# Retention and a multiplicative feed-forward layer on one core: where three pairs of weight sums are given out within one block

## The chip, the cores and the metric

The kernel runs on one core of a Trainium2 chip. The metric is the device time of one execution in microseconds (us). An execution agrees with the next within some tenths of a per cent, so differences under about 0.5% need several runs to be seen.

## The reference

All of it is float32. For 8 batches, 8 heads, 576 positions and 64 numbers per head, retention is computed without a softmax, and its output is the input of a feed-forward layer that multiplies two projections.

```python
scores = matmul(q, k.transpose(0, 1, 3, 2)) / sqrt(64)
ret = scores * where(i >= j, gamma[h] ** (i - j), 0)      # gamma = 1 - 2 ** (-5 - h)
x = matmul(ret, v)  ->  (4608 tokens, 512)
out = ((x @ w1) * (x @ w2)) @ w3 @ w_out                   # 512 -> 1024 -> 1024 -> 512
```

## The kernel before

**Attention in chunks.** Batches are taken in four pairs, and each sequence of 576 positions in five chunks (64 and four of 128). A step g is one chunk of one pair. `load` and `load_blocks` bring q, k and v; `front_blocks` turns q and k into qT and kT with VectorE transposes (L190); `score` (L233) multiplies them and VectorE applies the mask to the products (L236, tile pm, four instructions); `state` (L255) keeps the running sum over chunks; `pv_state` (L274) and `pv` (L299) make the output, which ScalarE copies into xT tiles of 384 tokens. The decays are multiplied onto q and v by GpSimd or ScalarE (L181, L202, L204).

**The feed-forward layer.** The two last weights are multiplied once into w3o. A token tile passes four `up` blocks, one for each quarter of the 1024 hidden columns, in which w1 and w2 are handled together, and then `down` blocks with w3o. Both are in a fast form with seven products for a 2 x 2 partition of the matrices instead of eight. Its operands are blocks of the weights (A11, A12, A22, kept in tile wA) and sums of them (S3 also in wA; S1, S2, S4 in wS), and blocks and sums of the tokens (B and T). There is one wA and one wS for each half of the hidden columns; these are the "first half" (wA0, wS0) and the "second half" (wA1, wS1).

**One up block** (`up`, L511 to L568) makes seven products in the order A11 x B11, S2 x T2, S3 x T3, S1 x T1, A22 x -T4, A12 x B21, S4 x B22. Each is eight matmuls (L528). A12 x B21 is added in PSUM onto the first product, and S4 x B22 onto the fourth. ScalarE copies the first product to tile c (L546, and L561 after A12 x B21), VectorE adds the others to c in five additions (`plus`, L533). The third addition reads the bank of S1 x T1; the fifth reads the same bank after S4 x B22. At the end VectorE multiplies the two projections into tile ab (L566).

**The down block** (`down`, L632 to L722, matmuls in L651) makes products 1, 7, 2, 6, 5, 4, 3 in this order. Its token sums S3, S2, S1 (L614, L618, L620) are put ahead of it, and S4 (L699) is made after product 2. VectorE combines the products (L701, L655), and the results are stored from L729. Product 2 is added onto product 1 in PSUM, and product 3 onto product 5, behind VectorE's addition of product 5.

**Work that is given out.** Lists of small jobs are filled ahead of a block, and each addition of a block hands one job from `aside` and one from `spread` to the engines:

```python
        def plus(ps, to, sb):
            nc.vector.tensor_add(c[:, to], ps, c[:, sb])
            convert(conv.pop(0) if isinstance(conv, list) else conv)
            for extra in (aside, spread):
                if extra:
                    extra.pop(0)()
```

The instructions of an engine stand in the order in which this code calls them. `flush` hands out all that is left in `spread`.

**Weight forms.** The first four token tiles use the seven-product form once. The later eight use it twice over (`up2`, matmuls in L1060), with weights that are read from device memory into a ring of slots (tile ra, `next_forms`, L961). `weight_forms(h, second)` makes these weights in place for half h, after the last up block that reads them. The first sums are one job, the second sums three. Each such job is a pair of VectorE instructions (L891), one on wA and one on wS. After the first sums, a job sends the results to the memory tile kept: four DMAs of wA (L901) and one of wS (L904), issued by GpSimd. The second sums change wA and wS again, so they wait until those sends have read them. After them a job sends the rest through SP's queue, eleven DMAs (L901, L904, L907). The first ring slot is laid over wA0, so its load stands behind these sends in SP's queue.

**The list around the change.** The four up blocks of the last tile that uses the one-level form, three down blocks and the jobs between them stand in the list `todo` (L1198 to L1202). `work(n)` runs the next n blocks from it, and after each block all jobs that follow it in the list. Up blocks 0 and 1 of the tile read the first half's weights, blocks 2 and 3 the second half's. The first half's first sums and their sends are given out in block 2, its second sums in block 3, the "last up block". In block 3, `aside` holds the transpose of the next chunk's query, an empty entry, the transpose of its key (L190), and then the down block's L614 and L618; L620 follows after the block.

Of the kernel before, what the change touches and what calls it, by code (L numbers as in the profile page):

```python
# [19 lines left out]
def kernel(  # L20
# [66 lines left out]
    def load(g, names, engine=nc.sync):  # L87
        i, c = divmod(g, NC)
        sz = sizes[c]
        src = {"k": k, "q": q, "v": v}  # L90
        for nm in names:
            t = pools["ld"].tile([P, 2 * H, D], F32, tag="ld_" + nm, name="ld_" + nm)
            engine.dma_start(
                t[:sz], src[nm][2 * i:2 * i + 2, :, starts[c]:starts[c] + sz, :].rearrange("b h p d -> p (b h) d"))
            live[nm, g] = t
# [64 lines left out]
    def load_blocks(g, nm):  # L160

        i, c = divmod(g, NC)
        n = sizes[c] // BL
        t = pools["ld"].tile([P, 2 * NP, P // BL, BL], F32, tag="ld_q", name="bl_" + nm)
        src = {"k": k, "q": q}[nm][2 * i:2 * i + 2].rearrange("b (p a) s d -> a (b p) s d", a=2)
        for a in range(2):
            for f in range(D // BL):
                part = (a * (D // BL) + f) * BL
                for m in range(n):
                    s0 = starts[c] + m * BL  # L170
                    nc.sync.dma_start(t[part:part + BL, :, m, :],
                                      src[a, :, s0:s0 + BL, f * BL:(f + 1) * BL].rearrange("m r x -> r m x"))
        live["bl_" + nm, g] = t

    def scale_blocks(g):
        c = g % NC
        n, n0 = sizes[c] // BL, starts[c] // BL
        t = live["bl_q", g]
        for b in range(2):
            part = t[:, b * NP:(b + 1) * NP, :n, :]  # L180
            nc.gpsimd.tensor_tensor(  # L181
                out=part, in0=part, in1=gqs[:, :, n0:n0 + n].unsqueeze(3).to_broadcast([P, NP, n, BL]),
                op=ALU.mult)

    def front_blocks(g, names="kq"):
        c = g % NC
        n = sizes[c] // BL
        for nm in names:
            dst = pools["fr"].tile([P, 2, NP, P], F32, tag=nm + "T", name=nm + "T", bufs=1 if nm == "k" else 2)
            nc.vector.transpose(  # L190
                dst[:, :, :, :sizes[c]].rearrange("p b m (n x) -> p (b m) n x", x=BL),
                live["bl_" + nm, g][:, :, :n, :])
            live[nm + "T", g] = dst

    def scale(g, nm, scalar=False, engine=nc.gpsimd):
        c = g % NC
        sz = sizes[c]
        t, gam = live[nm, g], {"q": gq, "v": gk}[nm]
        t = t[:sz].rearrange("p (b h) d -> p b h d", b=2)
        if scalar:  # L200
            for h in range(H) if scalar is True else scalar:
                nc.scalar.mul(t[:, :, h, :], t[:, :, h, :], gam[:sz, c, h:h + 1])  # L202
            return
        engine.tensor_tensor(  # L204
            out=t, in0=t, in1=gam[:sz, c].unsqueeze(1).unsqueeze(3).to_broadcast([sz, 2, H, D]), op=ALU.mult)

    def front(g, names="kq"):
        c = g % NC
        sz = sizes[c]
        for nm in names:  # L210
            src = live[nm, g]
            dst = pools["fr"].tile([P, 2, NP, P], F32, tag=nm + "T", name=nm + "T",
                                   bufs=1 if nm == "k" and g >= NC else 2)
            for b in range(2):
                tp = acc.tile([P, NP, P], F32, tag="acc", name="tp")
                for p in range(NP):
                    h = b * H + 2 * p
                    nc.tensor.transpose(tp[:, p, :sz],  # L218
                                        src[:sz, h:h + 2, :].rearrange("p a d -> p (a d)"),
                                        ident[:sz, :sz])  # L220
                nc.scalar.copy(dst[:, b, :, :sz], tp[:, :, :sz])
            live[nm + "T", g] = dst
# [55 lines left out]
    def pv(g):  # L278

        if ("xps", g) not in live:  # L280
            pv_state(g)
        i, c = divmod(g, NC)
        sz = sizes[c]
        live["x", g] = True
        vs, pm, banks = live["v", g], live["pm", g], live["xps", g]

        parts = []
        for n in range(NB):
            lo, hi = max(starts[c], n * TB), min(starts[c] + sz, (n + 1) * TB)
            if lo < hi:  # L290
                m = i * NB + n
                if ("xT", m) not in live:
                    live["xT", m] = xps[m % 4 == 3].tile([P, NP, 2, TB], F32, tag="xT", name="xT")
                parts.append((live["xT", m], lo - n * TB, lo - starts[c], hi - lo))
        for m, (b, n) in enumerate(bank_order):
            for r in range(2):
                for half in range(2):
                    p, j = 2 * r + n, half ^ r
                    nc.tensor.matmul(banks[r][heads[half], b, n, :sz], vs[:sz, b * H + 2 * p + j, :],  # L299
                                     pm[:sz, b, j, p, :sz], start=(c == 0 and m == 0), stop=True,  # L300
                                     skip_group_check=True)

        def evict():
            for x, to, fr, n in parts:
                for r in range(2):
                    nc.scalar.copy(  # L306
                        x[:, 2 * r:2 * r + 2, :, to:to + n].rearrange("p n b s -> p b n s"),
                        banks[r][:, :, :, fr:fr + n])

        return evict  # L310
# [261 lines left out]
    aside, owed, spread, beside, loads = [], [], [], [], []  # L572
# [256 lines left out]
    todo = [(0, 1, 2), (0, 0, 3), (0, 1, 3)] + [(0, 2, fp) for fp in range(NQ - 1)]  # L829
# [38 lines left out]
    todo = [(down, (0, 0), (0, 1)), (down, (0, 2), (1, 2))]  # L868
# [266 lines left out]
    def work(n):  # L1135
        while n > 0 and todo:
            fn, *args = todo.pop(0)

            nxt = next((x for x in todo if x[0] in real), None)
            if nxt and nxt[0] is down:  # L1140
                if fn is down:
                    args.append(nxt[1:])
                else:
                    ahead(*nxt[1:], 1 if fn is up2 else 3)
            if g == G and not todo:
                fn(*args, last=True)
            else:
                fn(*args)
            n -= 1
            while todo and todo[0][0] not in real:  # L1150
                todo.pop(0)[0]()
# [11 lines left out]
    for g in first_pair:  # L1163
        n = (1, 1, 2, 2)[g - NC]
        if not in_blocks[g + 2]:
            load(g + 2, "k")
            load_blocks(g + 2, "q")
        scale(g + 1, "v")
        if not in_blocks[g + 1]:
            front(g + 1, "k")  # L1170
            front_blocks(g + 1, "q")
        half = (n + 1) // 2
        if in_blocks[g + 1]:
            scale_blocks(g + 1)
            work(n - 1)
            aside.extend([lambda: front_blocks(g + 1, "q"), lambda: None, lambda: front_blocks(g + 1, "k")])
            work(1)
            while aside:
                aside.pop(0)()
            half = 0  # L1180
        if in_blocks[g + 2] and g + 2 < 2 * NC:
            load_blocks(g + 2, "q")
            load_blocks(g + 2, "k")
        work(half)
        if g < NC + 2:

            weight_forms(g - NC, False)[2]()
        pv(g)()
        load(g + 2, "v", nc.scalar if in_blocks[g + 2] else nc.sync)
        if in_blocks[g + 2] and (g + 2) % NC != NC - 1:  # L1190
            load(g + 2, "k")
        state(g + 1)
        score(g + 1)
        if not in_blocks[g + 2]:
            scale_blocks(g + 2)
        if g == NC + 1:
            list(strassen_tokens(1, 0))
            forms = [(lambda h=h, second=second: spread.extend(weight_forms(h, second)[:None if second else 2]),)  # L1198
                     for h in halves for second in (False, True)]
            ups = [(up, 1, 0, fp) for fp in range(NQ)]  # L1200
            todo.extend([*ups[:2], forms[0], ups[2], forms[1], ups[3], (flush,), forms[2], (flush,), (down, (1, 0), (1, 1)),
                         (down, (2, 2), (3, 2)), (open_second,), (down, (3, 0), (3, 1))])  # L1202
        if not in_blocks[g + 1]:
            work(n // 2)
# [116 lines left out]
```

## Time and profile before

| | |
|---|---|
| median of the runs shown (834.87, 837.93, 837.85) | 837.85 us |
| the profiled execution | 837.8 us, span 836.1 us |
| mean granted TensorE clock | 0.994 |
| TensorE matmuls busy | 817.3 us |
| VectorE busy | 548.1 us |
| last up block: start of the first of its matmuls, start of the next chunk's L274 | 305.36, 320.40 us |

In the profile a time is counted from the start of the span. PE is TensorE, PEld its weight loads, DVE is VectorE, ACT ScalarE, POOL GpSimd, SP the engine that only issues DMAs; a q behind the name stands for its queue. A row of the order of time has the start, the length, the engine, the line, the operation with the tiles it writes and reads, and in brackets the idle time of the engine before it and what ended that. A row of a stage has the busy time of each engine, then the granted clock as a share of full speed, the busy share of the 16 DMA engines (over 1 where transfers overlap in the records) and GB/s.

### The profile page before, as it was taken

The numbers are of one execution on the slowest core, as the hardware profiler recorded it, in microseconds if no ns is written. First come the engines' busy times: TensorE is split into PE (matmuls) and PEld (weight loads), VectorE is DVE, ScalarE is ACT, GpSimd is POOL, SyncE is SP. The second block draws the span as 40 slices with busy tenths as digits, with TensorE's granted clock in tenths as the row PEclk, the third lists the DMA queues.
The fourth block names the chain that finished last, engine by engine and source line by source line (L and its number), as shares of the span: only waits on it lengthen the run. The fifth ranks groups of instructions, "written<-read, shape, count | busy, mean of one in ns | idle before, by whom it ended". The sixth has DMA issues, their size and how long they took to land.

```text
span 836.1 us, 15815 instructions
## 1 busy us (share of the span) xinstructions
PE 817.3 (98%) x6117; PEld 737.0 (88%) x6117; DVE 548.1 (66%) x962; ACT 291.6 (35%) x609; POOL 222.4 (27%) x258
## 2 busy tenths in 40 slices
PE   8899999999999998999999999999999999999998
PEld 7789999744888997889999889998889998899987
DVE  4899999992554557664657765578745567645653
ACT  4787566581111111145443024342034331033300
POOL 1000000001304231115556105555005451045600
PEclk9999999999999998999999999999999999999999
DMA  9996464446247567977876437979155453045401
GB/s 187 222 217 147 78 144 134 114 114 109 93 78 197 101 157 232 241 219 182 218 219 181 112 81 200 219 240 225 52 102 177 146 208 113 33 151 202 151 25 51
DMA packets 196812, 126.96 MB, mean 152 GB/s; under 512 B 157848, under 2 KB 178456, under 8 KB 196736
## 3 DMA queue, kind: packets, MB, share of 16 engines
q1 hardware_dynamic: 168560, 50.40, 29.8%
q0 software_dynamic: 12480, 65.67, 24.1%
q10 hardware_dynamic: 15696, 9.87, 4.4%
q8 instruction: 48, 0.79, 0.4%
q14 instruction: 28, 0.23, 0.1%
HBM read 103.62 MB, written 22.28 MB: 151 GB/s over the span
## 4 chain that ended last, share of the span: by engine, by line
PE 88%; DVE 4%; DMA 3%; SPq 2%; issue 1%; ACT 1%; POOL 0%; ACTq 0%; DVEq 0%
PE po L651 25%; PE up L1060 17%; PE up L528 15%; PE seed L1060 13%; PE ps L477 7%; PE xps L299 4%; PE sc L233 3%; PE xps L274 2%; PE st L255 1%; PE tp L218 1%; DVE ab L1032 1%; DMA kept<-wS 1%; DMA ld_v<-in_v_dram 1%; DMA gk<-decay_k_dram 1%; DMA raw<-in_moe_w_dram 1%
## 5 line engine op out<-in xcount | busy, mean ns | idle before, releaser
L651 PE MATMUL po<-w3o,ab 128*128 128x256 f32 x552 | 124.9, 381 | 1.9 <-DVE pm L236 0.8
L651 PEld LDWEIGHTS po<-w3o,ab 128*128 128x128 f32 x552 | 103.7, 190 | 18.1 <-DVE ot L655 1.7
L1065 POOL TENSOR_TENSOR cc<-cc 128x384 f32<-128x384 f32 x112 | 109.4, 1003 | 3.8 <-ACT cc L1083 2.4
L1072 DVE TENSOR_TENSOR cc<-seed,cc 128x384 f32<-128x384 f32 x88 | 48.6, 552 | 69.1 <-PE seed L1060 59.4
L181 POOL TENSOR_TENSOR bl_q<-bl_q,gqs 128x512 f32<-128x512 f32 (+1 forms) x26 | 26.0, 1018 | 185.9 <-DMA bl_q<-in_q_dram 182.0
L1060 PE MATMUL up<-xT,ra 128*128 128x192 f32 x384 | 73.5, 328 | 0.0
L528 PE MATMUL up<-xT,wA 128*128 128x192 f32 x384 | 70.8, 328 | 1.0 <-ACT xT L306 1.0
L1072 DVE TENSOR_TENSOR cc<-up,cc 128x384 f32<-128x384 f32 x88 | 48.4, 550 | 30.2 <-PE up L1060 22.6
L533 DVE TENSOR_TENSOR c<-up,c 128x384 f32<-128x384 f32 x80 | 44.0, 550 | 36.7 <-PE up L528 36.3
L236 DVE TENSOR_TENSOR pm<-sc,mask 128x512 f32<-128x512 f32 (+1 forms) x80 | 45.3, 626 | 32.7 <-PE sc L233 32.6
L528 PEld LDWEIGHTS up<-xT,wA 128*128 128x128 f32 x384 | 63.3, 190 | 2.6 <-ACT xT L306 1.2
L651 PE MATMUL po<-wB,forms 128*128 128x256 f32 x288 | 65.1, 379 | 0.0
L1060 PEld LDWEIGHTS up<-xT,ra 128*128 128x128 f32 x384 | 63.8, 190 | 1.0
L961 POOL DMA_DIRECT2D ra<-kept x54 | 30.5, 565 | 118.7 <-PE seed L1060 95.8
L651 PEld LDWEIGHTS po<-wB,forms 128*128 128x128 f32 x288 | 54.7, 190 | 7.4
L1079 ACT COPY seed<-up 128x384 f32<-128x384 f32 x56 | 25.9, 463 | 100.2 <-PE up L1060 55.2
L477 PE MATMUL ps<-wo,w3T 128*128 128x512 f32 x128 | 55.1, 592 | 0.0
L1060 PE MATMUL up<-ra 128*128 128x192 f32 x288 | 54.7, 326 | 0.0
L1060 PE MATMUL seed<-e,ra 128*128 128x192 f32 x256 | 50.9, 329 | 0.0
L477 PEld LDWEIGHTS ps<-wo,w3T 128*128 128x128 f32 x128 | 24.3, 190 | 30.1 <-issue 29.7
L1060 PEld LDWEIGHTS up<-ra 128*128 128x128 f32 x288 | 48.1, 190 | 0.1
L528 PE MATMUL up<-T,wS 128*128 128x192 f32 x256 | 46.7, 326 | 1.1 <-DVE wS L149 1.1
(134 smaller groups left out, 1477.6 us busy)
## 6 DMA issues: line engine op xcount, KB each, us to landing
ra<-kept POOLq DMA_DIRECT2D x54, 896.0 KB, 5.0
raw<-in_moe_w_dram SPq DMA_DIRECT2D x72, 128.0 KB, 3.1
bl_q<-in_q_dram SPq DMA_DIRECT2D x192, 32.0 KB, 3.2
out_dram<-ot ACTq DMA_DIRECT2D x41, 128.0 KB, 2.3
bl_k<-in_k_dram SPq DMA_DIRECT2D x136, 32.0 KB, 3.4
raw<-in_moe_w_dram SPq DMA_DIRECT2D x16, 256.0 KB, 6.8
ld_k<-in_k_dram SPq DMA_DIRECT2D x8, 512.0 KB, 6.5
raw<-in_moe_w_out_dram SPq DMA_DIRECT2D x32, 128.0 KB, 2.7
```

Source lines behind the costliest of these rows:

```text
L181: nc.gpsimd.tensor_tensor(out=part, in0=part, in1=gqs[:, :, n0:n0 + n].unsqueeze(3).to_broadcast([P, NP, n, BL]), op=ALU.mult)
L236: nc.vector.tensor_mul(pm[:sz, b, j, :, :sz], sc[j][:sz, :, :sz], mask[:sz, :sz].unsqueeze(1).to_broadcast([sz, NP, sz]))
L299: nc.tensor.matmul(banks[r][heads[half], b, n, :sz], vs[:sz, b * H + 2 * p + j, :], pm[:sz, b, j, p, :sz], start=(c == 0 and m == 0), stop ...
L477: nc.tensor.matmul(ps, live["w3T", ft][:, g, :], live["wo"][:, g, :], start=(g == 0), stop=(g == KF - 1))
L528: nc.tensor.matmul(ps[:, w, :], a[:, w, r, :], b[:, r, :], start=(new and w == r == 0), stop=(w == r == 1), skip_group_check=True)
L533: nc.vector.tensor_add(c[:, to], ps, c[:, sb])
L651: nc.tensor.matmul(ps[nm], a[A][:, f, :], live["W"][B][:, f, :], start=(f == 0 and not on), stop=(f == NP - 1), skip_group_check=True)
L961: engine.dma_start(ring[n % 3], kept[n % 14 // 7][nm])
L1060: nc.tensor.matmul(ps[:, w, :], weight_of(slot, a, w), B[b], start=(new and w == 0), stop=True, skip_group_check=True)
L1065: nc.gpsimd.tensor_tensor(out=o, in0=o, in1=i, op=ALU.add)
L1072: nc.vector.tensor_add(c[:, j], ps, with_add[:, j])
L1079: nc.scalar.copy(p6, p1)
```

## The change

Two empty jobs are put into `spread` ahead of the three second sums of the first half. The last up block has five additions. Before, the three sums stand behind its first, second and third addition, and the sends behind its fourth. After the change, they stand behind the third, fourth and fifth, and the sends are handed out by the `flush` that follows the block. Nothing else differs.

```diff
             ups = [(up, 1, 0, fp) for fp in range(NQ)]
-            todo.extend([*ups[:2], forms[0], ups[2], forms[1], ups[3], (flush,), forms[2], (flush,), (down, (1, 0), (1, 1)),
+
+            later = (lambda: spread.extend([lambda: None] * 2),)
+            todo.extend([*ups[:2], forms[0], ups[2], later, forms[1], ups[3], (flush,), forms[2], (flush,), (down, (1, 0), (1, 1)),
                          (down, (2, 2), (3, 2)), (open_second,), (down, (3, 0), (3, 1))])
```

## The prediction

> **What bounds the kernel now.** I read the page first, then the waits, then the order of time around the change. The page says that TensorE is the bound nearly everywhere: it is busy for 98% of the span and makes 88% of the chain that ended last. So the change can only gain where TensorE stands still or runs slowly, and it moves work on VectorE.
>
> ```profile
> PE 817.3 (98%) x6117; PEld 737.0 (88%) x6117; DVE 548.1 (66%) x962; ACT 291.6 (35%) x609; POOL 222.4 (27%) x258
> PE 88%; DVE 4%; DMA 3%; SPq 2%; issue 1%; ACT 1%; POOL 0%; ACTq 0%; DVEq 0%
> ```
>
> In the waits, TensorE's longest single one of the whole run is 4.2 us, "PE up L528 <- DVE c L533"; no other reaches 1.5. The order of time for TensorE shows it in the last up block. Columns: start, length, line, and in brackets the idle time before and what ended it.
>
> ```profile
> 309.25 1.46 PE L528 MATMUL up<-T,wS 128*128 128x192 f32 x8
> 310.55 1.46 PE L528 MATMUL up<-T,wA 128*128 128x192 f32 x8
> 311.85 1.46 PE L528 MATMUL up<-xT,wA 128*128 128x192 f32 x8
> 317.55 2.93 PE L528 MATMUL up<-xT,wS 128*128 128x192 f32 x8 [4.23 <-DVE c L533]
> 320.40 1.98 PE L274 MATMUL xps<-qT,sb 64*64 64x128 f32 x32
> ```
>
> Products follow each other every 1.30 us, so the last one (S4 x B22) was due at 313.15 and began at 317.55. It adds to the PSUM bank that the block's third addition reads, so it waits for that addition. VectorE at the same time:
>
> ```profile
> 308.70 1.24 DVE L190 STREAM_TRANSPOSE qT<-bl_q 128x1024 f32<-128x1024 f32 x1
> 311.45 1.23 DVE L891 TENSOR_TENSOR wA<-wA 128x1024 f32<-128x1024 f32 x1 [1.51 <-DMA kept<-wA]
> 313.60 0.96 DVE L891 TENSOR_TENSOR wS<-wS 128x768 f32<-128x768 f32 x1 [0.92 <-DMA kept<-wS]
> 314.47 0.55 DVE L533 TENSOR_TENSOR c<-up,c 128x384 f32<-128x384 f32 x1
> ```
>
> The pair of sums behind the first addition (L891, in place) waits until the sends that GpSimd issued from 304.90 have read wA and wS (last one 307.93, landed 313.57). The second and third additions, whose products were long ready, are queued behind it. The third starts at 316.94.
>
> The gap costs more than itself. In the stages view (columns: busy us of PE, PEld, DVE, ACT, POOL, then granted clock, DMA share, GB/s):
>
> ```profile
> 313.00:315.40 2.40, 0.32 (x2) 0.02 (x1) 1.80 (x3) 0.48 (x1) 0.00 (x0) 1.00 0.01 1
> 315.40:322.20 6.80, 4.65 (x40) 4.00 (x40) 6.80 (x10) 0.00 (x0) 0.00 (x0) 0.50 0.25 75
> ```
>
> The clock is at half for 6.8 us. Against the block before it (products 288.73, L274 at 290.12, L299 at 291.15), the distance from S4 to L274 is 2.85 instead of 1.39 and from L274 to L299 1.92 instead of 1.03: 1.46 + 0.89 = 2.35 us. With the 4.40 us of the late start, **6.75 us** are lost here.
>
> **The change, part by part.** Nothing is added or removed: the same three pairs of sums and the same eleven sends. The order of the built programs differs on VectorE only. Behind the first addition no pair is left; the three pairs stand behind the third, fourth and fifth, and the sends come after the block. The order becomes: addition 1, transpose of the query, additions 2 and 3, transpose of the key (L190), pair, addition 4, L614, pair, addition 5, L618, pair, L566, the first pair of the second half, L620, then the four mask products (L236).
>
> *What goes.* Addition 2 can start when the query's transpose ends (308.70 + 1.24 = 309.94). Addition 3 needs its product (309.25 + 1.46 = 310.71) and is done by some 311.4. S4 is due at 313.15 and finds it done. So the gap and with it the half clock go: -6.75 us.
>
> *What is late next.* VectorE now meets the key's transpose at 311.4, whose loads (L171 on SP, 300.96 + 9.34 = 310.30 at the last issue) are still moving:
>
> ```profile
> 300.96 9.34 SPq L171 DMA_DIRECT2D bl_k<-in_k_dram  x16
> ...
> 312.00:313.30 1.30, 1.30 (x9) 1.02 (x7) 0.68 (x1) 0.00 (x0) 0.00 (x0) 1.00 0.60 162
> 313.30:320.00 6.70, 2.47 (x9) 2.42 (x8) 6.40 (x8) 0.48 (x1) 0.00 (x0) 0.66 0.01 1
> ```
>
> Up to here both kernels send the same transfers, and none moves after 313.3. The sum on wS that waited for GpSimd's send began 0.5 us after that queue's last bytes (313.1, then 313.60). So I put the transpose at **313.9**; bounds 313.4 (no delay) and 314.8 (the loads' own median of 5.1 us from the last issue). This wait replaces those on the sends, which have landed by then.
>
> From there VectorE has no idle time. The distances from start to start in the rows of before: transpose 1.15, wA 1.13, wS 0.87, addition 0.47, L614 or L618 0.60, L566 0.87, L620 0.60. Up to the first mask product that is 1.15 + 4 x 2.00 + 2 x 0.47 + 3 x 0.60 + 0.87 = 12.76, so it starts at 326.66 and ends, at 0.68, at 327.34. Before it was 326.14: VectorE, which idles 3 us later on, gains nothing, and TensorE runs into it.
>
> - Score (L233): the key is ready at 315.1, L233 is due at 324.21 - 6.75 = 317.46. No wait.
> - Down block (L651): product 1 needs additions and L614 (318.2, due 319.4): no wait. Product 6 needs L618 (321.3, due 324.7): no wait. Product 5 writes a bank that the first mask product must have read. In before it begins at 331.48 + 1.73 = 333.21, so it is due at 326.46 and waits till 327.39: **+0.93**.
> - Product 3 adds onto product 5's bank, behind the addition of product 5. VectorE: masks end at 326.66 + 2.47 = 329.1, then L699 0.60, L701 0.46, one addition 0.34, L614 0.60, the addition 0.42: 331.52. Product 3 is due at 336.66 - 6.75 + 0.93 = 330.84: **+0.70**.
>
> Sum: -6.75 + 0.93 + 0.70 = **-5.1 us** at the next chunk's L274 (338.48 becomes 333.4). Each 1 us of the transpose's start is 1 us of the result, so its bounds give -5.6 and -4.2. With no wait left at all it is -6.75.
>
> *What else is moved.* The third pair's wA sum starts 7.29 us after the transpose, at 321.2, so SP's sends start at some 322.4 instead of 319.77. Behind them in SP's queue stand four loads and the first ring load (L961, issued from 339.21, landing 11.3 us later): all 2.6 us later, the ring at some 353. Its first reader is the first matmul on ra at 370.52 - 5.1 = 365.4, so 12 us of cover. GpSimd's sends of the second half wait for a sum that starts at 324.1 instead of 323.5; the last (328.04, landing up to 8.2) is read 0.5 us later, at 336.8. The second half's next pairs, due at 338.93 - 5.1 = 333.8, will wait for it, about 3 us on VectorE. Queued behind them is L699 of the next down block, needed when its product 2 ends (346.90 - 5.1 = 341.8); the pairs end at about 339.7. That cover is 2 us; if it is gone, each further us reaches TensorE only after another 1.1 us of idle time before L701.
>
> After 340 no row shows TensorE waiting for a transfer; its waits there are 0.3 to 1.2 us and on VectorE or ScalarE. So the shift should last to the end. The profiled execution took 837.8 (span 836.1 and 1.7 around it), and the median of the runs shown is 837.85, the same. **837.8 - 5.1 = 832.7.**
>
> [...] The clock row shows half speed 2.1 us after the last matmul (313.31 to 315.45). [...]
>
> **The rivals.**
>
> *The waits vanish (831.0).* If VectorE reaches the masks 1 us earlier than I work out, both new waits go: 837.8 - 6.75. For it: they are sums of many small distances. Against it: the loads' last bytes at 313.3 are a floor, which leaves 0.4 at least of the first wait.
>
> *Less is kept (834 to 836).* The lowest run shown, 834.87, is 3 us below the others, about the 2.35 us of the half clock, so the gap may cost other executions only 4.4; then 4.4 - 1.6 = 2.8 is won against them. The same size comes out if the key's loads land at 314.8 and the second half's pairs outrun their 2 us of cover by another 1.4 (5.1 - 0.9 - 1.4 = 2.8). For it: TensorE will depend on a VectorE that is full for 15 us. Against it: the clock row, and DMA at rest after 313.3.
>
> *It does not do what it says (837.8).* If S4 waited for something behind the third addition too, the gap would stay. Against it: the wait names L533, and in the new order nothing but the query's transpose precedes additions 2 and 3.
>
> *Slower (841.6).* The sums run at the slow rate. One row shows it: L891 at 299.42 took 2.48 us instead of 1.2 while GpSimd ran L204 (298.92 to 300.82). Four pairs now stand between the key's transpose and the masks. If every instruction of them doubled, 4 x (1.27 + 0.95) = 8.9 us would come on top of product 5's wait: -5.1 + 8.9 = +3.8. It decides from 57% of them on. Against it: GpSimd computes nothing from 310 to 325, and only issues DMAs until 334; the masks beside those issues took their usual 2.47.
>
> **How the numbers follow.** Forecast, 831.7 to 833.5: 0.55. Waits vanish: 0.13. Less is kept: 0.24. No effect: 0.04. Slower: 0.04. A difference under 0.5% (4.19 us, so 833.66 to 842.04) is about what a measurement of this kernel cannot tell from no change. Faster is the first two, 0.68; same is the third and fourth, 0.28; slower is 0.04, though its own forecast is near the bound. The range runs from a little under the second case to the upper part of the third: 830.8 to 835.4.
>
> **What would show it.** In the profile after: S4 directly behind its predecessor near 313.2; granted clock 1.00 from 310 to 335; the key's transpose with an idle time before it, ended by bl_k, near 313.9; no L891 wait on kept in this block; L236 near 326.7; L651 waiting for L236 for 0.9 and for L655 for 0.7; L274 of the next chunk near 333.4; L891 of the second half waiting for kept near 334. It is wrong if the transpose starts after 314.8, if the clock falls again at the two short waits, or if TensorE waits for ra or in the down blocks after 340 where it did not.

## The result

The changed kernel takes 831.61 us (median of 8 executions, 830.01 to 834.30) against 836.36 us before (median of 8, 834.87 to 837.93). The ratio is 0.9947 with a 95% interval of 0.9931 to 0.9963, so it is faster by 4.4 us, between 3.1 and 5.8; the two medians lie 4.75 us apart. The profiled execution took 832.77 us, its span is 831.0 us instead of 836.1, and its mean granted clock 0.999 instead of 0.994. Of what the kernel before lacks to 1, two thirds are the half clock of 6.8 us in the last up block; the rest is one of 3.4 us near its start (15.06 to 18.47).

The order of time of TensorE after the change, in the last up block and the down block behind it (start, length, line, operation, and in brackets idle time and what ended it):

```profile
305.43 1.46 PE L528 MATMUL up<-xT,wA 128*128 128x192 f32 x8
...
311.93 1.46 PE L528 MATMUL up<-xT,wA 128*128 128x192 f32 x8
313.23 1.46 PE L528 MATMUL up<-xT,wS 128*128 128x192 f32 x8
...
324.82 1.89 PE L651 MATMUL po<-wB,forms 128*128 128x256 f32 x8
327.37 1.99 PE L651 MATMUL po<-wB,forms 128*128 128x256 f32 x8 [0.65 <-DVE pm L236]
329.20 1.89 PE L651 MATMUL po<-wB,ab 128*128 128x256 f32 x8
331.49 1.99 PE L651 MATMUL po<-w3o,ab 128*128 128x256 f32 x8 [0.40 <-DVE ot L655]
333.41 1.10 PE L274 MATMUL xps<-qT,sb 64*64 64x128 f32 x32
```

The last product of the up block, S4 x B22, now follows its predecessor after the usual 1.30 us. In its place there are two short waits in the down block, at products 5 and 3. VectorE in the same stretch:

```profile
309.94 0.52 DVE L533 TENSOR_TENSOR c<-up,c 128x384 f32<-128x384 f32 x1
310.83 0.56 DVE L533 TENSOR_TENSOR c<-up,c 128x384 f32<-128x384 f32 x1 [0.38 <-PE up L528]
313.87 1.25 DVE L190 STREAM_TRANSPOSE kT<-bl_k 128x1024 f32<-128x1024 f32 x1 [2.48 <-DMA bl_k<-in_k_dram]
...
326.63 2.48 DVE L236 TENSOR_TENSOR pm<-sc,mask 128x512 f32<-128x512 f32 x4
```

Additions 2 and 3 (L533) are done by 311.4. VectorE then waits 2.48 us for the loads of the key, and has no idle time from there to the masks (L236). The clock (the column behind the five engines, here 1.00) stays up in the stage in which it was at half before:

```profile
315.40:322.20 6.80, 6.80 (x88) 6.05 (x81) 6.80 (x9) 1.57 (x5) 0.00 (x0) 1.00 0.19 42
```

For what follows one measure is used, because the profiles differ by up to 3.3 us in when they reach the block (303.54 to 306.84 us): **the block's length**, from the first matmul of the last up block to the L274 behind the down block. The prediction and the expectations call that L274 the next chunk's; the table of the time before gave this name to the one ahead of the down block (320.40). In the kernel before it is this row:

```profile
338.48 1.10 PE L274 MATMUL xps<-qT,sb 64*64 64x128 f32 x32
```

The length is 338.48 - 305.36 = 33.12 us before and 333.41 - 305.43 = 27.98 us after, 5.14 less. From that L274 to the end of the span both take the same, 497.62 and 497.59 us, so nothing is given back later.

### The profile page after: what moved, and what is told of

Same layout as the page of the kernel before. It is cut to its first block, busy times and chain, and to the rows that moved or that the text cites. A ratio compares the mean times of both kernels' runs of the same rounds, so it can differ in the third digit from the quotient of the medians.

```text
span 831.0 us, 15815 instructions
## 1 busy us (share of the span) xinstructions
PE 817.5 (98%) x6117; PEld 737.0 (89%) x6117; DVE 547.6 (66%) x962; ACT 291.8 (35%) x609; POOL 222.3 (27%) x258
## 4 chain that ended last, share of the span: by engine, by line
PE 89%; DVE 6%; DMA 2%; issue 1%; SPq 1%; ACT 1%; ACTq 0%; POOL 0%; DVEq 0%; POOLq 0%
PE po L651 24%; PE up L1060 17%; PE up L528 14%; PE seed L1060 13%; PE ps L477 7%; PE xps L299 3%; PE sc L233 3%; PE xps L274 2%; PE tp L218 2%; PE st L255 1%; SPq L171 1%; DVE pm L236 1%; DVE ab L1032 1%; PE idle L131 1%; DMA ld_v<-in_v_dram 1%
## 5 line engine op out<-in xcount | busy, mean ns | idle before, releaser
L1060 PE MATMUL up<-xT,ra 128*128 128x192 f32 x384 | 73.7, 328 | 0.1
L236 DVE TENSOR_TENSOR pm<-sc,mask 128x512 f32<-128x512 f32 (+1 forms) x80 | 45.4, 627 | 35.1 <-PE sc L233 35.1
L533 DVE TENSOR_TENSOR c<-up,c 128x384 f32<-128x384 f32 x80 | 44.1, 552 | 36.7 <-PE up L528 35.7
L1060 PEld LDWEIGHTS up<-xT,ra 128*128 128x128 f32 x384 | 63.7, 190 | 1.4 <-DMA ra<-kept 0.4
L1060 PE MATMUL up<-ra 128*128 128x192 f32 x288 | 54.7, 326 | 0.0
L1060 PE MATMUL seed<-e,ra 128*128 128x192 f32 x256 | 50.9, 329 | 0.0
L1060 PEld LDWEIGHTS up<-ra 128*128 128x128 f32 x288 | 48.1, 190 | 0.1
```

Of the source, the lines that this page charges most:

```text
L236: nc.vector.tensor_mul(pm[:sz, b, j, :, :sz], sc[j][:sz, :, :sz], mask[:sz, :sz].unsqueeze(1).to_broadcast([sz, NP, sz]))
L1060: nc.tensor.matmul(ps[:, w, :], weight_of(slot, a, w), B[b], start=(new and w == 0), stop=True, skip_group_check=True)
```

## The experiments

**Theory A**: the gap came because the third addition stood on VectorE behind a pair of sums that waited for GpSimd's sends. What TensorE meets now is VectorE's row of work that begins with the key's transpose. **Rivals**: the gain is the half clock alone (B); the two waits that came back are not from VectorE's row (C); it matters only that no pair stands behind the first addition (D); the pairs' own time makes the gap and not their wait (E); a later place is better as such (F). G and H ask how often the half clock comes.

**The changed kernel again** (no edit).

> The changed kernel once more, so that the others of this group have it on the same chip. Theory A (the third addition stood behind a pair of sums that waited for the sends; now VectorE's row of work from the key's transpose on is what TensorE meets): profile as before, S4 directly behind its predecessor, L236 near 326.6, span near 831; the timed median 4 to 5 us below the kernel before. Theory B (the gain depends on the half clock alone, so an execution without it gains little): the kernel before shows clocks of 0.999 in some executions and the difference to those is under 3 us.

Measured: 832.28 us (median of 6) against 836.00 before, ratio 0.9955 (0.9942 to 0.9967). The medians lie 3.7 us apart, less than the 4 to 5 expected. Block 27.43 us. The sharper reading is in the key's transpose:

```profile
313.65 1.25 DVE L190 STREAM_TRANSPOSE kT<-bl_k 128x1024 f32<-128x1024 f32 x1 [1.94 <-DMA bl_k<-in_k_dram]
333.18 1.10 PE L274 MATMUL xps<-qT,sb 64*64 64x128 f32 x32
```

It started 8.44 us after the block's first matmul in the profile above and 7.90 here, and from it to the L274 behind the down block it is 19.54 and 19.53 us. So the loads' landing decides, one us for one us, as theory A has it; two more profiles below say the same. Theory B asked for a clock of 0.999 in some executions of the kernel before. The eleven beside this run show 0.994 to 0.998, so it is left to the three profiles further down.

**The pair ahead of the key's transpose.**

```diff
-            for extra in (aside, spread):
+            for extra in ((spread, aside) if "swap" in live else (aside, spread)):
...
-            later = (lambda: spread.extend([lambda: None] * 2),)
+            later = (lambda: (spread.extend([lambda: None] * 2), live.update(swap=True)),)
-            todo.extend([*ups[:2], forms[0], ups[2], later, forms[1], ups[3], (flush,), forms[2], (flush,), (down, (1, 0), (1, 1)),
+            todo.extend([*ups[:2], forms[0], ups[2], later, forms[1], ups[3], (lambda: live.pop("swap"),), (flush,), forms[2], (flush,), (down, (1, 0), (1, 1)),
```

> The changed kernel with the two hands of an addition exchanged in the last up block alone: the pair of sums goes ahead of the key's transpose, so that the wA sum fills VectorE's idle time before the loads land. Theory A: the wA sum starts at some 311.5, the wS sum still at 313.6 to 313.9 (send landed), the key's transpose at 314.5 and the first mask product at 325.2 instead of 326.6. The two waits of the down block (0.65 and 0.40) go or shrink to 0.2, and the next chunk's L274 comes at 332.4: 1.0 us less than the changed kernel, 6 us less than the kernel before in the profile. Rival C (the two waits come from something else than VectorE's row, or the wS sum meets a later landing): the same time as the changed kernel, within 0.3.

Measured: 831.00 us (median of 5), 1.3 below the changed kernel beside it and 5.0 below the kernel before; ratio 0.9934 (0.9921 to 0.9947), block 26.39 us. VectorE, in the order of time:

```profile
311.60 1.22 DVE L891 TENSOR_TENSOR wA<-wA 128x1024 f32<-128x1024 f32 x1
313.50 0.96 DVE L891 TENSOR_TENSOR wS<-wS 128x768 f32<-128x768 f32 x1 [0.68 <-DMA kept<-wS]
314.37 1.24 DVE L190 STREAM_TRANSPOSE kT<-bl_k 128x1024 f32<-128x1024 f32 x1
...
325.12 2.48 DVE L236 TENSOR_TENSOR pm<-sc,mask 128x512 f32<-128x512 f32 x4
```

And TensorE's down block, with both waits gone:

```profile
325.12 3.62 PE L651 MATMUL po<-wB,forms 128*128 128x256 f32 x16
328.57 1.89 PE L651 MATMUL po<-wB,ab 128*128 128x256 f32 x8
330.30 1.89 PE L651 MATMUL po<-w3o,ab 128*128 128x256 f32 x8
332.12 1.10 PE L274 MATMUL xps<-qT,sb 64*64 64x128 f32 x32
```

The wA sum fills 1.22 us of the wait for the key, and the masks come 1.3 us earlier than in this group's profile of the changed kernel (326.40). Rival C falls: the two waits were VectorE's row.

**One empty job instead of two.**

```diff
-            later = (lambda: spread.extend([lambda: None] * 2),)
+            later = (lambda: spread.extend([lambda: None]),)
```

> One empty job instead of two: the pairs stand behind additions 2, 3 and 4, so the third addition waits behind one pair, and that pair waits for the sends as in the kernel before. Theory A: addition 2 at 309.9, wA sum at 311.5, wS sum at 313.6, addition 3 at 314.5, S4 at 315.1 instead of 313.2, a gap of some 1.8 us; L236 at 325.7, so the two waits in the down block are gone. If the clock stays up through a gap of 1.8, the next L274 is at 333.6, 0.2 us later than in the changed kernel (time 4.9 us below before); if the clock falls to half as it did in the 4.2 us gap, it is at 336, only 2.5 below before. Rival D (it matters only that the sends' wait is not behind the first addition): no gap here.

Measured: 832.05 us (median of 4), ratio 0.9952 (0.9939 to 0.9965), block 27.77 us, 0.2 below the changed kernel's 27.98 and 0.3 above its 27.43. The time is 3.95 us below before and not 4.9. The gap is there and small, and the clock stays up (1.57 us for the eight matmuls behind the gap, against 2.93 at half):

```profile
310.04 1.46 PE L528 MATMUL up<-xT,wA 128*128 128x192 f32 x8
312.61 1.57 PE L528 MATMUL up<-xT,wS 128*128 128x192 f32 x8 [1.11 <-DVE c L533]
```

The late start is 2.57 - 1.30 = 1.27 us, less than the 1.9 expected, because the sends landed 7.6 us after the block's first matmul and not 8.2. The waits of the down block are gone. So this place trades the two waits for a gap of their size. Rival D falls.

**The sends read other tiles.** The kernel before in its own order; in `weight_forms` the first half's first sends read the second half's wA and wS.

```diff
-                    x = wA[h][:, r, :, :, m * QC + f * P:m * QC + f * P + P]
+                    x = wA[h if second or not m else 1][:, r, :, :, m * QC + f * P:m * QC + f * P + P]
...
-                    engine.dma_start(to, wS[h][:, :, m].rearrange("p a j c n -> p a (j c n)"))
+                    engine.dma_start(to, wS[h if second or not m else 1][:, :, m].rearrange("p a j c n -> p a (j c n)"))
```

> The kernel before, in its own order, but the first half's first sends read the second half's wA and wS, which nothing writes until later; the same transfers, and the first pair waits for no send. (The first half's stored weights are then partly the second half's, so the output is another one.) Theory A, which splits the loss of 4.40 us into queueing behind two pairs and waiting for the sends: the first pair starts at 309.9, addition 2 at 311.9, the second pair to 314.4, addition 3 at 314.4, S4 at 315.0: a gap of 1.7 us and not 4.2, L236 at 323.6 and no wait in the down block. Time 4.9 us below before if the clock stays up, 2.5 below if it falls to half. Rival E (the two pairs' own time ahead of the third addition makes the gap, the wait for the sends does not): the gap stays near 4 us and the time near that of before.

Measured: block 28.25 us, that is 4.87 less than before; 833.19 us (median of 4), ratio 0.9963 (0.9950 to 0.9976). VectorE and TensorE:

```profile
310.54 1.18 DVE L891 TENSOR_TENSOR wA<-wA 128x1024 f32<-128x1024 f32 x1
311.64 0.95 DVE L891 TENSOR_TENSOR wS<-wS 128x768 f32<-128x768 f32 x1
312.50 0.55 DVE L533 TENSOR_TENSOR c<-up,c 128x384 f32<-128x384 f32 x1
...
314.97 0.55 DVE L533 TENSOR_TENSOR c<-up,c 128x384 f32<-128x384 f32 x1
```

```profile
312.53 1.46 PE L528 MATMUL up<-xT,wA 128*128 128x192 f32 x8
315.58 1.57 PE L528 MATMUL up<-xT,wS 128*128 128x192 f32 x8 [1.58 <-DVE c L533]
```

The late start is 315.58 - 312.53 - 1.30 = 1.75 us. This splits the 4.40 us of the kernel before: 1.75 is the queue behind two pairs of sums, 2.65 the wait of the first pair for its sends. Rival E falls for the larger part. The time fell by 2.8 us only, not 4.9. Against the changed kernel beside it the block is 0.8 us longer (28.25 against 27.43) and the median 0.9 (833.19 against 832.28), so the shortfall lies with the kernel before: by the timed medians it does not lose as much as in its profile.

**Three empty jobs.** The edit is that of one empty job, with 3. The second group ran on another chip.

> Three empty jobs instead of two: the pairs stand behind additions 4 and 5 and after the block. Theory A: VectorE does the same work from the key's transpose to the first mask product, in another order, so L236 starts 12.8 us after that transpose as in the changed kernel, the down block has the same two short waits, and from the block's first matmul to the next chunk's L274 it is 27.4 to 28.0 us as in the changed kernel's two profiles; time within 0.3 us of the changed kernel. Rival F (a later place is better, the earlier pairs still hold additions up): a further gain of 0.5 us or more.

Measured: 832.33 us (median of 4), ratio 0.9939 (0.9915 to 0.9962), block 27.32 us; the key's transpose 7.78 us after the first matmul, and 19.54 from it to the next L274. The same row of work in another order takes the same time; rival F falls by the block's length. In time it can be compared by the ratio alone, since the changed kernel was not run on this chip.

**The kernel before, three more profiles** (no edit).

> The kernel before, another profile. The timed medians show 3.7 to 4.8 us between the two kernels, the two profiles 5.1. Theory G: the half clock after the gap does not come in every execution, because where the gap falls against the clock's own period differs. Then some looks have a granted clock of 1.00 in the last up block and 30.8 us from its first matmul to the next chunk's L274, and others half clock and 33.1. Rival H: the half clock comes each time (33.1 in every look), and the difference between timed and profiled lies ahead of the block, in the start of the execution.

> The kernel before, a further profile for the same question: 30.8 us or 33.1 us from the first matmul of the last up block to the next chunk's L274, with the clock at full or at half speed behind the gap.

> The kernel before, a further profile for the same question: 30.8 us or 33.1 us from the first matmul of the last up block to the next chunk's L274, with the clock at full or at half speed behind the gap.

Measured: blocks of 29.76, 30.22 and 31.36 us, none as long as the 33.12 of the profile that I predicted from. S4 x B22 in the first, second and third of them:

```profile
316.39 1.57 PE L528 MATMUL up<-xT,wS 128*128 128x192 f32 x8 [3.10 <-DVE c L533]
```

```profile
317.12 1.57 PE L528 MATMUL up<-xT,wS 128*128 128x192 f32 x8 [3.56 <-DVE c L533]
```

```profile
315.67 2.78 PE L528 MATMUL up<-xT,wS 128*128 128x192 f32 x8 [3.08 <-DVE c L533]
```

Two had the clock at full behind the gap (1.57 us for the eight matmuls), one at half (2.78). The late start was 3.26, 3.72 and 3.24 us instead of 4.40, since the last send landed 7.1 to 7.6 us after the first matmul (its wS sum started then) and not 8.2. So theory G holds as to how often the clock falls, in two of four profiles (its cause is not shown), and the landing time adds to it, which neither G nor H had. H falls, since the half clock did not come each time. Theory B is half right: the two blocks without a half clock are 1.8 to 2.8 us longer than those of the changed kernel (27.43 to 27.98), so the gap alone is worth that much and the half clock comes on top.

How much a timed execution loses is left open. The blocks of these four profiles are 3.3 us longer on average than the three of the changed kernel, and what lies ahead of the block and behind it agrees to 0.1 us; but the three executions (834.83 to 835.37 us) are all faster than the seven timed beside them (835.53 to 838.79), so they do not stand for those.

**The better order again, with the changed kernel beside it**, in a third group on another chip (no further edit).

> The version with the pair ahead of the key's transpose once more, beside the changed kernel on another chip, since 1 us is near what the medians can tell. Theory A: 26.3 to 26.5 us from the block's first matmul to the next chunk's L274, no wait in the down block, and a median 0.7 to 1.6 us below the changed kernel's. If the gain of the first group was chance, the medians lie within 0.4 us.

> The changed kernel as the neighbour for the run before. Theory A: 27.3 to 28.0 us from the block's first matmul to the next chunk's L274, 1 us of it in two short waits of the down block, and as much longer as the key's transpose starts later after the block's first matmul (19.5 us between that start and the next L274 in each profile so far).

Measured: 830.31 us (median of 5) against 832.26 (median of 5) for the changed kernel; ratios to the kernel before 0.9915 (0.9903 to 0.9927) and 0.9944 (0.9930 to 0.9958), which do not overlap. Blocks 26.48 and 27.98 us. In the changed kernel the transpose again starts 8.44 us after the first matmul and the next L274 19.54 us later. So the pair ahead of the key's transpose beats both kernels, by 7.3 us against before in this group, and its blocks of 26.39 and 26.48 us are about the 26.37 (33.12 - 6.75) that are left when every loss of the profile before is taken out.

## Why the prediction was right

- *The time.* The forecast was 832.7, the median 831.61: inside the range, and just under the 831.7 at which the main case began. Two errors partly cancel. The base of 837.85 was 1.5 us above the median of eight executions (836.36), and the gain of 5.1 was 0.35 above the 4.75 between the medians. The time alone could not tell the main case from "the waits vanish" (831.0); the two waits in the profile do.
- *The bound and what goes.* S4 x B22 was to start near 313.2 and did at 313.23; the clock stayed at 1.00.
- *What is late next.* The key's transpose was put at 313.9, between 313.4 and 314.8; it started at 313.87 with the wait for bl_k in front. The 12.76 us from it to the masks were 12.76 (326.63). That the start came within 0.03 us is partly luck, since in the four profiles in which the transpose waits for the loads it lies 7.78 to 8.44 us after the block's first matmul. The chain that ended last runs through it; columns are start, us and what:

```profile
308.93 4.92 DMA bl_k<-in_k_dram
313.85 0.02 issue
313.87 0.03 DVE kT L190
```

- *The two waits.* Product 5 was to be 0.93 late and product 3 another 0.70. By starts they were 327.37 - 324.82 - 1.73 = 0.82 and 331.49 - 329.20 - 1.73 = 0.56. Restarting after a wait cost about 0.1 us both times (1.83 us instead of 1.73 from product 5 to the next, 1.92 instead of 1.82 from product 3 to L274), which the sum did not have and which makes up for it: L274 at 333.41, forecast 333.4.
- *What else is moved.* SP's sends start at 322.39 (forecast 322.4). The ring load was issued at 344.83 and not 2.6 us later than 339.21: the sends and loads ahead of it took longer in the queue (22.44 us from the first send to this issue, 19.44 before). Its cover of 12 us hid that: the first matmul on ra started at 365.44, forecast 365.4, without a wait. The second half's pairs were to wait 3 us for their sends; they waited 0.51 (335.58), since the last send landed by then, 7 us after its issue at 328.53 and not 8.2. They ended at 338.55, and L699 was reached with 3.28 us of idle time in hand. One sign of being wrong did come: a wait of 0.4 us for a ring load appears near 547, where there was none. It cost nothing, since the wait on VectorE beside it fell from 0.84 to 0.45, and it is not due to the change, since the three further profiles of the kernel before show such waits too (weight loads of L1060 on xT and ra, 0.5, 0.2 and 0.7 us).
- *The size that was off.* The term "6.75 us are lost here" is right for the one profiled execution and too large for the others: in three more the block lost 3.4 to 5.0 us (29.76, 30.22, 31.36 against 26.39). That fits a measured 4.4 us instead of 5.1 but is not shown to be the cause, since the interval of 3.1 to 5.8 holds both. The half clock itself was missing in two of four profiles. Of the rivals, "less is kept" had this reason, that the half clock does not come every time, and missed the second one, that the landing of the sends moves by 1.1 us (8.2 and 7.1 us after the block's first matmul). "Slower" fell with its condition: the sums on wA beside no GpSimd computation took 1.18 to 1.22 us each, those on wS 0.95.

## What to carry to other kernels

VectorE took its jobs in the order of the program: in the profile before, the second addition stood behind a sum that waited for a send until 313.60, with its product long ready. So the sum that waited for a transfer held back the ready additions behind it, the second until 314.47 and the third until 316.94; when such jobs are given out between others, put first those that another engine waits for, and behind them what fills the time until the transfer lands. After a wait is taken out, walk down the moved engine's row to its next reader, since the same work ends at about the same moment unless idle time was filled (here the masks began at 326.14 before, at 326.63 after, and at 325.12 where a sum filled the idle time). And do not price a wait from one profile when it hangs on a transfer's landing or on the clock: look at several (here the landing moved by 1.1 us between profiles, and the clock fell in two of four).

## What was not expected of the hardware

The half clock behind the gap lasted 6.8 us in one profile and 3.4 in another (granted clock 0.50 from 315.43 to 322.26, and from 315.86 to 319.28). Idle times of 4.23 and 3.08 us were followed by it, 3.10 and 3.56 were not, and 1.58 and 1.11 were not. So the length of the gap does not decide alone.

| profile | idle time of TensorE | S4 x B22 starts | clock falls to half | clock is back |
|---|---|---|---|---|
| before | 4.23 | 317.55 | 315.43 | 322.26 |
| third further one of before | 3.08 | 315.67 | 315.86 | 319.28 |
| first further one of before | 3.10 | 316.39 | no | |
| second further one of before | 3.56 | 317.12 | no | |
| the sends read other tiles | 1.58 | 315.58 | no | |
| one empty job | 1.11 | 312.61 | no | |

The clock fell 2.12 us ahead of the start of S4 x B22 in the first of these and 0.19 us behind it in the second, and it was back 4.71 and 3.61 us after that start. The second further profile has a stage of 3.5 us in which TensorE did nothing and the clock was at 1.00:

```profile
313.60:317.10 3.50, 0.00 (x0) 0.00 (x0) 3.50 (x6) 0.48 (x1) 0.00 (x0) 1.00 0.00 0
```

In the profile before, the clock changes at 15.06, 18.47, 315.43 and 322.26. These moments lie 3.413, 296.96 and 6.827 us apart, which is 1, 87 and 2 times 3.413 us; the two changes in the third further one lie 3.42 us apart. That fits theory G, by which it matters where the gap falls against the clock's own period. But what decides whether the clock falls behind a gap is not shown by these few cases.
